# Copying and storing the last 128-token groups one at a time, on two DMA queues

## The chip, the cores and the metric

One core of one Trainium2 chip. The metric is the time of one execution in microseconds (us). Each run's time is about 1.8 us above the span that its trace shows, so the two are not mixed below: "time" is the metric, "span" is the trace. In the views PE is TensorE, PEld its weight loads, ACT ScalarE, DVE VectorE, POOL GpSimd and SP SyncE; a q behind a name (SPq, ACTq) is the sequencer of that engine, which issues DMAs and waits for semaphores.

## The reference, cut to what matters

```python
def _attn_ref(x):                      # x: 8 x 3008 x 256, f32
    X = np.fft.fft(np.fft.fft(x, axis=1), axis=2)
    return X.real
def _moe_ref(x, w_gate, w_val, w_out): # 24064 tokens, 256 -> 1536 -> 256
    gate = np.maximum(x @ w_gate, 0.0)
    val = x @ w_val
    return gate * val @ w_out
```

The kernel works in 24 blocks of tokens (8 batches, 3 blocks each). A block yields 512 tokens and, by the symmetry of the transform, 512 mirrored tokens. The output matmul handles them in groups of 128 tokens.

## The kernel before

The parts that matter. PSUM is the memory that TensorE writes its results to, in banks of 2 KB per partition. `pso` is a PSUM pool of two buffers; a tile `po` of 128 x 2 x 256 f32 (2 KB per partition, one bank) takes two groups, `s` even and `s` odd. `sg` is 0 for the plain half of a block and 1 for the mirrored one.

```python
pso = ctx.enter_context(tc.tile_pool(name="pso", bufs=2, space=PS))
...
def out_piece(t, half):
    b, blk, f = steps[t]
    for k in range(8 * f + 4 * half, 8 * f + 4 * half + 4):
        gi, ff = divmod(k, NF)                       # NF = 12 matmuls per group
        sg, s = divmod(gi, 4)
        g = 3 - s if sg else s
        if s == 0 and ff == 0:
            state["os"] = op.tile([128, 4, D], F32, tag="os", name="os")
        if s % 2 == 0 and ff == 0:
            state["po"] = pso.tile([128, 2, D], F32, tag="o", name="po")
        po, os_ = state["po"], state["os"]
        nc.tensor.matmul(po[:, s % 2, :], lhsT=..., rhs=wo[:, ff, :],
                         start=(ff == 0), stop=(ff == NF - 1))          # L539
        if s % 2 == 1 and ff == NF - 1:
            nc.scalar.copy(os_[:, s - 1:s + 1, :], po[:])               # L542
        if s == 3 and ff == NF - 1:
            store(b, blk, sg, os_)

def store(b, blk, sg, os_):                          # four stores, all on SyncE
    for u in range(4):
        ka = NKA * u + 4 * blk
        src = os_[32 * u:32 * u + 32].rearrange("p g d -> p (g d)")
        ...
        lo = 1 if ka + 3 == 47 else 0
        hi = 3 if ka == 0 else 4
        row = b * S + NA - ka - 3 + lo
        nc.sync.dma_start(out=view(out, row * D, [[NA * D, NB], [1, (hi - lo) * D]]),
                          in_=src[:, lo * D:hi * D])                    # L557
```

The framework that builds the program inserts the semaphores. It orders accesses of different engines to one PSUM tile, and the DMAs of SyncE and ScalarE take their completion semaphore in turn from one set of eight, whichever of the two queues they are on. A DMA is issued only when the DMA that had its semaphore before has landed.

## Time and profile before

| kernel before | |
|---|---|
| time, first 3 runs | 660.69 us median (660.03 to 661.86) |
| span of the profiled run | 660.6 us |
| TensorE busy | 637.0 us, 96% |
| after the last output matmul | 4.9 us |

First the head of the page: the busy time of each engine, and the first line of the chain that ended last.

```profile
span 660.6 us, 12759 instructions
...
PE 637.0 (96%) x4266; PEld 410.1 (62%) x4266; DVE 553.3 (84%) x871; ACT 426.7 (65%) x809; POOL 468.8 (71%) x630
...
PE 81%; POOL 11%; DVE 5%; issue 2%; ACT 1%; POOLq 0%; DVEq 0%
```

TensorE (PE) is the limit of the kernel: nearly always busy, and most of the chain. The change does not touch what it does in the body of the program. It acts at the end, so here is the timeline of the end. Columns: start, duration, engine, line and operation, output and input, count of merged instructions, and in brackets the idle time before the first of them with what ended it.

```profile
644.85 0.36 PE L521 MATMUL V<-pq,wm 128*128 128x480 bf16 x1
...
645.05 10.64 PE L539 MATMUL po<-wo,h 128*128 128x256 bf16 x96
...
653.16 0.58 ACT L542 COPY os<-po 128x512 f32<-128x512 f32 x1 [2.08 <-PE po L539]
655.73 0.58 ACT L542 COPY os<-po 128x512 f32<-128x512 f32 x1 [1.99 <-PE po L539]
656.34 1.72 SPq L557 DMA_DIRECT2D out_dram<-os  x4
```

All the work that remains after 645.05 us is 96 output matmuls, which run as one unbroken row to 655.7. A copy of 128x512 follows, then four stores that SyncE (SP) issues one after another. How their packets moved is in the windows of that stretch (window, its length, busy time of each engine, granted clock, share of the DMA engines, GB/s):

```profile
656.32:657.16 0.84, 0.00 (x0) 0.00 (x0) 0.00 (x0) 0.00 (x0) 0.00 (x0) 1.00 0.00 0
657.16:659.27 2.11, 0.00 (x0) 0.00 (x0) 0.00 (x0) 0.00 (x0) 0.00 (x0) 1.00 0.91 233
659.27:660.60 1.33, 0.00 (x0) 0.00 (x0) 0.00 (x0) 0.00 (x0) 0.00 (x0) 1.00 0.00 0
```

Last, the closing of the program: SyncE checks one semaphore after another, then drains, and all engines shake hands. The line of its drains:

```profile
L642 SPq DRAIN  x3: 7/7/7, 659.8 to 660.1; - x3
```

The first drain came at 659.8 and the end at 660.6; this last 0.84 us is the same in every trace below.

**A yardstick for what follows.** Runs of one kernel differ by 2 to 3 us (those of own_banks below by 4.9), which is more than this tail can yield. In the traces of kernels that differ only in the tail, the start of the last L521 matmul (the last line of work before the row of 96) lies anywhere from 642.9 to 645.8 us. So I read the *tail* of each trace: from the start of that matmul to the end of the span. Before it is 660.6 - 644.85 = 15.75 us.

### The profile page before, as it was taken

The numbers are of one execution on the slowest core, as the hardware profiler recorded it, in microseconds if no ns is written. First come the engines' busy times: TensorE is split into PE (matmuls) and PEld (weight loads), VectorE is DVE, ScalarE is ACT, GpSimd is POOL, SyncE is SP. The second block draws the span as 40 slices with busy tenths as digits, with TensorE's granted clock in tenths as the row PEclk, the third lists the DMA queues.
The fourth block names the chain that finished last, engine by engine and source line by source line (L and its number), as shares of the span: only waits on it lengthen the run. The fifth ranks groups of instructions, "written<-read, shape, count | busy, mean of one in ns | idle before, by whom it ended". The sixth has DMA issues, their size and how long they took to land.

```text
span 660.6 us, 12759 instructions
## 1 busy us (share of the span) xinstructions
PE 637.0 (96%) x4266; PEld 410.1 (62%) x4266; DVE 553.3 (84%) x871; ACT 426.7 (65%) x809; POOL 468.8 (71%) x630
## 2 busy tenths in 40 slices
PE   6789999999999999999999999999999999999997
PEld 3424666665666666666666666666656666666665
DVE  9857688888788887989888887988979898899991
ACT  5465676775667766676676766676666766666662
POOL 9639579959975599658995599756996355455451
PEclk9799999999999999999999999999999999999999
DMA  9792472393126721196114922177111241211113
GB/s 252 239 202 51 127 202 78 85 234 104 42 78 142 192 82 49 41 196 190 40 53 106 226 81 69 51 161 221 41 42 49 67 118 39 81 33 43 51 32 94
DMA packets 32294, 70.76 MB, mean 107 GB/s; under 512 B 4475, under 2 KB 21491, under 8 KB 30227
## 3 DMA queue, kind: packets, MB, share of 16 engines
q1 hardware_dynamic: 29892, 58.16, 32.3%
q0 software_dynamic: 2336, 11.80, 9.0%
q8 instruction: 33, 0.54, 0.3%
q14 instruction: 33, 0.26, 0.1%
HBM read 39.77 MB, written 30.96 MB: 107 GB/s over the span
## 4 chain that ended last, share of the span: by engine, by line
PE 81%; POOL 11%; DVE 5%; issue 2%; ACT 1%; POOLq 0%; DVEq 0%
PE po L539 33%; PE V L495 9%; PE V L493 8%; PE G L472 8%; PE G L471 8%; PE G L483 8%; POOL h L509 3%; POOL eo L102 3%; POOL xl L99 2%; PE V L521 2%; PE ps L162 2%; POOL eo L130 2%; DVE E L503 1%; PE psw L261 1%; PE ps L204 1%
## 5 line engine op out<-in xcount | busy, mean ns | idle before, releaser
L509 POOL TENSOR_TENSOR h<-gm,E 128x480 bf16<-128x480 f32 (+1 forms) x225 | 276.0, 1227 | 147.5 <-DVE E L517 128.2
L539 PE MATMUL po<-wo,h 128*128 128x256 bf16 x2304 | 333.5, 272 | 0.0
L539 PEld LDWEIGHTS <-h 128*128 128x128 bf16 x2304 | 222.7, 98 | 88.2 <-issue 3.9
L486 ACT ACTIVATE gm<-G 128x480 f32<-128x480 f32 (+1 forms) x288 | 167.3, 581 | 141.8 <-PE G L483 112.1
L497 DVE TENSOR_TENSOR h<-gs,V 128x512 bf16<-128x512 f32 x288 | 193.9, 686 | 32.6 <-PE V L495 22.0
L503 DVE SCALAR_TENSOR_TENSOR E<-nb,af,V 128x480 f32<-128x480 bf16 (+1 forms) x225 | 163.0, 724 | 16.4 <-PE V L493 10.5
L473 ACT ACTIVATE gs<-G 128x512 f32<-128x512 f32 x288 | 171.5, 595 | 0.8 <-PE G L472 0.8
L517 DVE SCALAR_TENSOR_TENSOR E<-E,V 128x480 f32<-128x480 f32 (+1 forms) x225 | 148.1, 658 | 0.0
L483 PE MATMUL G<-pq,wm 128*128 128x480 bf16 (+1 forms) x288 | 106.6, 370 | 7.8 <-ACT gs L473 7.7
L495 PE MATMUL V<-pq,ws 128*128 128x512 bf16 x288 | 109.0, 378 | 1.1 <-DVE E L503 0.5
L472 PE MATMUL G<-pq,ws 128*128 128x512 bf16 x288 | 109.1, 379 | 0.4 <-DVE pq L209 0.4
L471 PE MATMUL G<-pq,wc 128*128 128x512 bf16 x288 | 109.1, 379 | 0.0
L493 PE MATMUL V<-pq,wc 128*128 128x512 bf16 x288 | 109.1, 379 | 0.0
L542 ACT COPY os<-po 128x512 f32<-128x512 f32 x96 | 56.2, 586 | 58.4 <-PE po L539 58.4
L509 DVE TENSOR_TENSOR h<-gm,V 128x480 bf16<-128x480 f32 (+1 forms) x63 | 41.9, 665 | 39.3 <-ACT gm L486 33.8
L102 POOL TENSOR_TENSOR eo<-xl 94x381 bf16<-94x381 f32 x70 | 69.0, 992 | 0.4
L99 POOL TENSOR_TENSOR xl<-xl,xh 94x765 f32<-94x765 f32 x35 | 63.2, 1806 | 2.7
L495 PEld LDWEIGHTS <-ws 128*128 128x128 bf16 x288 | 28.1, 98 | 33.9
L472 PEld LDWEIGHTS <-ws 128*128 128x128 bf16 x288 | 28.1, 98 | 31.5 <-issue 0.2
L172 ACT CAST t<-ps 96x512 bf16<-96x512 f32 x63 | 36.9, 585 | 6.6 <-PE ps L160 5.4
L493 PEld LDWEIGHTS <-wc 128*128 128x128 bf16 x288 | 28.1, 98 | 14.8 <-issue 7.0
L471 PEld LDWEIGHTS <-wc 128*128 128x128 bf16 x288 | 28.1, 98 | 13.1 <-issue 9.7
(106 smaller groups left out, 346.0 us busy)
## 6 DMA issues: line engine op xcount, KB each, us to landing
out_dram<-os SPq DMA_DIRECT2D x176, 128.0 KB
xl<-in_x_dram SPq DMA_DIRECT2D x7, 1360.0 KB
Td<-t SPq DMA_DIRECT2D x7, 768.0 KB
t<-Td SPq DMA_DIRECT2D x7, 768.0 KB
nb<-Nd SPq DMA_DIRECT2D x24, 128.0 KB
xl<-in_x_dram SPq DMA_DIRECT2D x7, 238.0 KB
xl<-in_x_dram SPq DMA_DIRECT2D x4, 384.0 KB
xh<-in_x_dram SPq DMA_DIRECT2D x4, 384.0 KB
```

Of the source, the lines that this page charges most:

```text
L471: nc.tensor.matmul(e["G"][:], lhsT=wc[0][:, fs], rhs=pq[:, 0, :], start=True, stop=False)
L472: nc.tensor.matmul(e["G"][:], lhsT=ws[0][:, fs], rhs=pq[:, 1, :], start=False, stop=True)
L473: nc.scalar.activation(e["gs"][:], e["G"][:], ACTF.Relu)
L483: nc.tensor.matmul(e["G"][:, cols], lhsT=wm[0][:, f * 128:(f + 1) * 128], rhs=pqt[b, blk][:, 1, cols], start=False, stop=True, skip_group_ ...
L486: nc.scalar.activation(e["gm"][:, cols], e["G"][:, cols], ACTF.Relu)
L493: nc.tensor.matmul(e["V"][:], lhsT=wc[1][:, fs], rhs=pq[:, 0, :], start=True, stop=split(t))
L495: nc.tensor.matmul(e["V"][:], lhsT=ws[1][:, fs], rhs=pq[:, 1, :], start=False, stop=True, skip_group_check=split(t))
L497: nc.vector.tensor_tensor(e["h"][:, 0, :], e["gs"][:], e["V"][:], op=ALU.mult)
L503: nc.vector.scalar_tensor_tensor(e["E"][:, cols], nbt[b, blk][:, cols], af[:, f:f + 1], e["V"][:, cols], op0=ALU.mult, op1=ALU.add)
L509: eng.tensor_tensor(free(e["h"][:], 512 + cols.start + NB - 1, [NB, (cols.stop - cols.start) // NB], [-1, NB]), e["gm"][:, cols].rearrange ...
L517: nc.vector.scalar_tensor_tensor(e["E"][:, cols], e["E"][:, cols], 2.0, e["V"][:, cols], op0=ALU.mult, op1=ALU.subtract)
L539: nc.tensor.matmul(po[:, s % 2, :], lhsT=ht[t - f + ff]["h"][:, sg, g * 128:(g + 1) * 128], rhs=wo[:, ff, :], start=(ff == 0), stop=(ff == ...
```

## The change

Intent: shorten what follows the last matmul. The last 128 tokens need not wait to be copied and stored together with the 384 before them, and two engines can issue the stores faster than one.

```diff
-            if s % 2 == 1 and ff == NF - 1:
+            if ff < NF - 1:
+                continue
+            if t - f == len(steps) - NF and sg == 1:
+                nc.scalar.copy(os_[:, s:s + 1, :], po[:, s % 2:s % 2 + 1, :])
+                store_last(b, blk, os_, s)
+                continue
+            if s % 2 == 1:
                 nc.scalar.copy(os_[:, s - 1:s + 1, :], po[:])
-            if s == 3 and ff == NF - 1:
+            if s == 3:
                 store(b, blk, sg, os_)
+
+    def store_last(b, blk, os_, s):
+        for u in range(4):
+            ka = NKA * u + 4 * blk
+            if s == 0 and ka + 3 == 47:
+                continue
+            (nc.sync if u % 2 else nc.scalar).dma_start(
+                out=view(out, (b * S + NA - ka - 3 + s) * D, [[NA * D, NB], [1, D]]),
+                in_=os_[32 * u:32 * u + 32, s, :])
```

More of the change, by code (lines that the diff above doesn't have):

```diff
@@ L540, in out_piece @@
                              rhs=wo[:, ff, :], start=(ff == 0), stop=(ff == NF - 1))
-            if s % 2 == 1 and ff == NF - 1:
+            if ff < NF - 1:
[5 more added lines that the diff above has]
+            if s % 2 == 1:
                 nc.scalar.copy(os_[:, s - 1:s + 1, :], po[:])
-            if s == 3 and ff == NF - 1:
+            if s == 3:
                 store(b, blk, sg, os_)
+    def store_last(b, blk, os_, s):
[4 more added lines that the diff above has]
+            (nc.sync if u % 2 else nc.scalar).dma_start(
+                out=view(out, (b * S + NA - ka - 3 + s) * D, [[NA * D, NB], [1, D]]), in_=os_[32 * u:32 * u + 32, s, :])
     def store(b, blk, sg, os_):
```

## The prediction

> **What bounds the kernel now.** TensorE. The page has PE busy 96% of a 660.6 us span, and 81% of the chain that ended last is PE. In the windows from 560 to 640 us PE is always busy, at a granted clock of 1.00. The change leaves that alone. It acts only on the mirrored half of the last block, after about 650 us.
>
> **That tail before (timeline of the last 20 us).** 96 output matmuls run without a pause, one per 0.109 us (12 per group of 128 tokens, 1.31 us). The last ends at 655.71. One copy of 128x512 takes 0.585 (655.73 to 656.32). SyncE issues four stores of 128 KB in 1.72 us (656.34 to 658.06). Their packets run from 657.16 to about 659.2, the wait for the fourth ends at 659.64, the closing handshake at 660.6. So 4.9 us follow the last matmul: copy 0.6, stores 3.3, closing 1.0.
>
> **What the change does to it.**
> - *Shorter last copy.* 128x256 in place of 128x512. ACT's forms 128x480 and 128x512 differ by 27 ns for 32 columns (0.84 ns each), so I estimate 0.37 us: **-0.21**.
> - *Fewer issues behind it.* Two on each of two queues, not four on one. Starts on SyncE were 0.36 to 0.46 apart; the last issue now starts about 0.4 instead of 1.31 after the copy: **-0.9**.
> - *Less data behind it.* 128 KB, not 512; each store 32 KB. The fourth store took 2.0 us from issue to landing; the one-row store to Nd released its reader 1.1 us after its issue. I estimate 1.6: **-0.4**.
> - *New waits of TensorE.* Each pair of groups shares one PSUM tile of one bank. Until now the copy came after both. Now the copy of group 0 reads the bank before the matmuls of group 1 write its other half, likewise 2 and 3. The Trainium skill (PSUM — Partial Sum Buffer, "PSUM bank collisions raise a hardware error") says that two engines must be kept apart per bank and quadrant, not per address, so I expect the second group to wait for the copy. The trace before has no such wait on po. Cost: the last matmul starts at 655.42 and lands at 655.71 (0.18 more than its pitch), copy 0.37, release of PE about 0.05 (seen for gs): about 0.62 each, twice, both on the only chain: **+1.24**.
> - *More issues*, 15 stores of 1 KB rows instead of 4 of 4 KB: the first 11 hide behind later matmuls. A first use of ScalarE for stores has no trace here: **+0 to 0.3**.
>
> The skill (DMA: Bandwidth & Descriptors, "Issuing engines are not separate DMA queues") says that a second issuing engine saves only issue time, all I credit it with. -1.5 and +1.3 to +1.5 cancel: about -0.2 us. The whole tail after the last matmul is 0.7%, so 2% can't come from here.
>
> **Predicted: 660.5 us, 659.1 to 661.6 in 8 of 10. Faster by over 2%: 0.005; within 2%: 0.99; slower: 0.005.**
>
> **What would show it.** Two idle gaps of PE of about 0.6 us before an output matmul, released by the ACT copy; last matmul ending near 656.95; copies of about 0.37; last copy ending near 657.3; two issues per queue within 0.9 us of it; last landing about 2 us after the copy (3.3 before). Everything before about 648 us the same.
>
> **What would make it wrong.** No gap (halves not ordered): then about 659.2. ScalarE's issues slow, its queue's first use costly, or stores waiting for earlier ones' semaphores: up to 661.5. Runs differ by 1.8 us anyway.

## The result, and the profile after

| | before | after |
|---|---|---|
| time, median of 6 runs | 661.28 us (660.03 to 662.0) | 661.12 us (660.25 to 661.8) |
| ratio | | 0.9995, 95% interval 0.9979 to 1.0012 |
| tail in the trace | 15.75 us | 15.9 us |

A ratio is the mean time of one kernel's runs over the mean of the other's runs of the same rounds, so it is not quite the ratio of the medians.

No difference in time can be seen. The profiled run of the changed kernel has a span of 658.8 us, 1.8 us less than the one of before, but that is not the change: it had reached the last L521 matmul 1.98 us earlier. The head of its page:

```profile
span 658.8 us, 12777 instructions
...
PE 636.7 (97%) x4266; PEld 409.9 (62%) x4266; DVE 552.7 (84%) x871; ACT 426.7 (65%) x811; POOL 468.8 (71%) x630
...
PE 74%; POOL 11%; DVE 6%; DMA 4%; issue 3%; ACT 1%; SPq 0%; POOLq 0%; DVEq 0%; ACTq 0%
```

Busy times are those of before. The 4% of DMA in this chain come mostly from one load of x at 282 us, where the backward walk took another branch; the change is nowhere near it. The end is what differs:

```profile
642.87 0.36 PE L521 MATMUL V<-pq,wm 128*128 128x480 bf16 x1
...
643.08 6.71 PE L539 MATMUL po<-wo,h 128*128 128x256 bf16 x60
...
649.87 0.37 ACT L544 COPY os<-po 128x256 f32<-128x256 f32 x1 [0.77 <-PE po L539]
650.27 0.89 ACTq L558 DMA_DIRECT2D out_dram<-os  x2
650.29 2.78 PE L539 MATMUL po<-wo,h 128*128 128x256 bf16 x24 [0.50 <-ACT os L544]
...
652.32 3.97 SPq L558 DMA_DIRECT2D out_dram<-os  x7
653.11 0.37 ACT L544 COPY os<-po 128x256 f32<-128x256 f32 x1 [0.94 <-PE po L539]
...
653.53 1.47 PE L539 MATMUL po<-wo,h 128*128 128x256 bf16 x12 [0.46 <-ACT os L544]
...
655.04 0.37 ACT L544 COPY os<-po 128x256 f32<-128x256 f32 x1 [1.56 <-PE po L539]
655.44 0.87 ACTq L558 DMA_DIRECT2D out_dram<-os  x2
```

The row of 96 matmuls is broken twice: 60, then 24, then 12. Each break is ended by the copy of the first group of a pair (`<-ACT os L544`). The bracket says 0.50 and 0.46 because it counts from the modelled end of the matmul before; from start to start the breaks are 0.776 and 0.732, and the usual pitch is 0.109, so they cost 0.667 and 0.623, **1.29 us** together.

Two more lines. The waits of SyncE over the last 20 us (who waited for what: us in total, times, longest), and its drains:

```profile
SPq L558 <- DMA out_dram<-os: 2.6, 4, 1.4
```

```profile
L657 SPq DRAIN  x3: 7/7/7, 657.9 to 658.2; - x3
```

The first says that stores waited for *earlier stores to land*: they share the eight semaphores. Such waits were not there before, where the only waits of SyncE for a store were those of the closing. The second is the closing, to which I return.

So the sum of the tail, taken from the single records of both traces (us):

| piece | before | after | difference |
|---|---|---|---|
| L521 to end of last copy | 11.46 | 12.53 | +1.07 (waits of PE +1.29, shorter copy -0.21) |
| end of last copy to last landing | 3.32 | 2.08 | -1.24 |
| last landing to SyncE's first drain | 0.13 | 0.43 | +0.30 |
| drain to end | 0.84 | 0.84 | 0 |
| tail | 15.75 | 15.88 | +0.13 |

"Landing" is the moment at which SyncE's wait for that store's semaphore is released. (From the rounded lines shown above, the tail after is 658.8 - 642.87 = 15.93; the records give 15.88.) The +0.30 has a plain cause: at the end SyncE checks the eight semaphores in a fixed order at about 0.06 us each. Before, the store that landed last was last but one in that order; after, it was second, and six checks of long-finished stores followed it.

### The profile page after: what moved, and what is told of

Same layout as the page of the kernel before. It is cut to its first block, busy times and chain, and to the rows that moved or that the text cites. A ratio compares the mean times of both kernels' runs of the same rounds, so it can differ in the third digit from the quotient of the medians. Undisturbed runs are those within 1.5% of the kernel's fastest.

```text
span 658.8 us, 12777 instructions
## 1 busy us (share of the span) xinstructions
PE 636.7 (97%) x4266; PEld 409.9 (62%) x4266; DVE 552.7 (84%) x871; ACT 426.7 (65%) x811; POOL 468.8 (71%) x630
## 4 chain that ended last, share of the span: by engine, by line
PE 74%; POOL 11%; DVE 6%; DMA 4%; issue 3%; ACT 1%; SPq 0%; POOLq 0%; DVEq 0%; ACTq 0%
PE po L539 30%; PE V L495 8%; PE V L493 7%; PE G L472 7%; PE G L471 7%; PE G L483 7%; POOL h L509 4%; POOL eo L102 4%; DMA xh<-in_x_dram,ix 3%; POOL xl L99 3%; PE V L521 2%; PE ps L162 2%; DVE E L503 1%; DVE h L497 1%; PE psw L261 1%
```

## The experiments

The theory: the change does shorten what follows the last copy, and the copies that split a pair give it back, because both groups of a pair lie in one PSUM bank. (A bank of its own always means a tile of its own here, so no run separates the bank from the tile; "bank" below stands for both.) Rivals: the breaks cost nothing because the stores set the end; the stores gain nothing because their transfers are at a floor; the copies cost by their number and not by the bank. Except where a full timing is given, only tails are compared. The parts of all the tails stand together at the end of this section.

### copies_only: the cost alone

Against the changed kernel:

```diff
-                store_last(b, blk, os_, s)
+                if s == 3:
+                    store(b, blk, sg, os_)
```

> The cost side alone: the four single copies of the change, but the old four stores of 128 KB on SyncE after the last. The tail is read from the start of the last value matmul on wm (PE V, 15.75 us before the end in the kernel before, 15.93 in the changed one). Theory (a copy makes TensorE wait because both groups of a pair lie in one PSUM bank): two PE gaps of 0.62 to 0.67 us beyond the pitch, last copy 0.37, stores as before: tail 15.75 + 1.29 - 0.21 = 16.8. Rival (the gaps are swallowed, the end is set by the stores' own pace): tail 15.5 to 15.8.

Tail 16.83 us, as the theory had it. Both breaks are there, and the four stores behave as in the kernel before (last landing 3.33 us after the copy). Timeline:

```profile
652.15 2.78 PE L539 MATMUL po<-wo,h 128*128 128x256 bf16 x24 [0.51 <-ACT os L544]
...
655.39 1.47 PE L539 MATMUL po<-wo,h 128*128 128x256 bf16 x12 [0.46 <-ACT os L544]
...
656.90 0.37 ACT L544 COPY os<-po 128x256 f32<-128x256 f32 x1 [1.56 <-PE po L539]
657.29 1.71 SPq L573 DMA_DIRECT2D out_dram<-os  x4
```

The breaks lie on the only chain there is: they move the end by their full length, less 0.21 for the shorter copy.

### own_banks: the cost taken away

Against the changed kernel, a PSUM tile for each of the last four groups:

```diff
-            if s % 2 == 0 and ff == 0:
+            if ff == 0 and (s % 2 == 0 or (sg == 1 and t - f == len(steps) - NF)):
```

> The change, with a PSUM tile of its own for each of the last four groups. Bank theory: no PE wait for a copy, last matmul 1.29 us earlier than in the change relative to the anchor (10.8 instead of 12.1 us after it). If only the bank matters the tail is 15.93 - 1.29 = 14.6. Second theory, from the list of waits in the program: the 15 stores share 8 completion semaphores in turn over both queues, and with the groups 1.3 us apart the two last stores on SyncE have to wait for landings of stores that ScalarE issued 0.4 us or less earlier (the very last one for a store of its own group), so the last landing comes about 3.3 us after the last copy instead of 2.1 and the tail is 15.6 to 15.9, the gain lost again. Times: within 0.3% of before in either case.

Tail 15.62. Time 660.71 us median (660.14 to 665.05), before 661.33 on the same chip, ratio 0.9998 (0.9973 to 1.0023): no difference. The 96 matmuls are one row again, so the bank was the cause of the breaks, and the last copy ends 1.27 us earlier than in the changed kernel, measured from L521. But the last landing now comes 3.09 us after it instead of 2.08. The timeline, and the waits of SyncE:

```profile
643.47 10.64 PE L539 MATMUL po<-wo,h 128*128 128x256 bf16 x96
...
649.52 1.72 SPq L566 DMA_DIRECT2D out_dram<-os  x4
...
650.67 0.91 ACTq L558 DMA_DIRECT2D out_dram<-os  x2
...
653.27 3.18 SPq L558 DMA_DIRECT2D out_dram<-os  x7
654.16 0.37 ACT L544 COPY os<-po 128x256 f32<-128x256 f32 x1 [0.93 <-PE po L539]
```

```profile
SPq L558 <- DMA out_dram<-os: 2.1, 2, 2.0
```

This is the size that the second theory of the expectation gave. The list of waits in the built program for the last two stores on SyncE is (output of the program listing, not of the profile; the number after DMAHW names one of the eight semaphores):

```
297 L558 DMACopy out_0_dram<-os_8984 32x256 [waits DMAHW0_49,Activation_49]
298 L558 DMACopy out_0_dram<-os_8984 32x256 [waits DMAHW1_49]
```

DMAHW1 had been given to the first store of the same group, which ScalarE issued at 0.03 us after the copy. SyncE was released from this wait at 1.60 us after the copy, when that store had landed, and only then issued the very last store. But the expectation had named only such waits at the end, and this one cost at most 0.2 us: the issue before it had ended at 1.41. The long wait, 2.0 us, came earlier. SyncE's first small store (of the first group) had the semaphore of a store of the same group that ScalarE had issued, the second of the two at 650.67, and could be issued, at 653.27, only when that one had landed. From then on SyncE issued its seven stores 0.42 to 0.57 us apart, so that those of the last group stood at the end of a full queue.

So most of the gain of 1.29 us was lost again: 1.01 us of later landing, through waits for shared semaphores and the queue that the first of them backed up. No run removes the early wait alone.

### own_banks_3_1: fewer stores, so fewer waits for semaphores

As own_banks, with the first three groups stored together after group 2 (four stores of 3 KB rows), the last one alone:

```diff
                 nc.scalar.copy(os_[:, s:s + 1, :], po[:, s % 2:s % 2 + 1, :])
-                store_last(b, blk, os_, s)
+                if s >= 2:
+                    store_last(b, blk, os_, 0 if s == 2 else 3, s + 1)
```

(`store_last` here takes a range of groups, as in pair_copies below.)

> As own_banks, but the first three groups are stored together (four stores of 3 KB rows after group 2), the last group alone: 8 stores instead of 15, so no store of the last group waits long for an earlier one (at most about 0.2 us for one). Both theories of own_banks together: no PE wait, last landing about 2.1 to 2.3 us after the last copy, tail 14.6 to 15.0, 0.7 to 1.1 us less than before (0.1 to 0.17% of the time, so perhaps not clear of noise). If semaphores don't matter it equals own_banks.

Tail 15.00, at the edge of what was expected. Last landing 2.54 us after the copy: one store on SyncE still waited 0.7 us for an earlier one, more than the 0.2 that I had worked out. Time 661.64 us median (660.95 to 662.4), ratio 0.9999 (0.9983 to 1.0015): timing does not resolve it.

### pair_copies: the benefit alone

Against the changed kernel:

```diff
-                nc.scalar.copy(os_[:, s:s + 1, :], po[:, s % 2:s % 2 + 1, :])
-                store_last(b, blk, os_, s)
+                if s % 2 == 1:
+                    nc.scalar.copy(os_[:, s - 1:s + 1, :], po[:])
+                    store_last(b, blk, os_, s - 1, s + 1)
...
-    def store_last(b, blk, os_, s):
+    def store_last(b, blk, os_, s0, s1):
...
-            if s == 0 and ka + 3 == 47:
-                continue
+            lo = s0 + 1 if s0 == 0 and ka + 3 == 47 else s0
             (nc.sync if u % 2 else nc.scalar).dma_start(
-                out=view(out, (b * S + NA - ka - 3 + s) * D, [[NA * D, NB], [1, D]]), in_=os_[32 * u:32 * u + 32, s, :])
+                out=view(out, (b * S + NA - ka - 3 + lo) * D, [[NA * D, NB], [1, (s1 - lo) * D]]),
+                in_=os_[32 * u:32 * u + 32, lo:s1, :].rearrange("p g d -> p (g d)"))
```

> The benefit side without the split of the copies: one copy of 128x512 per pair as before, four stores of 2 KB rows per pair, alternating between the two queues. No PE wait (matmuls as before). Last landing about 2.2 to 2.5 us after the copy instead of 3.3, closing up to 0.3 longer: tail 14.7 to 15.1. Rival (the queue and the size gain nothing because the transfers are at their floor): tail 15.6 to 15.8.

The end in the timeline:

```profile
655.58 0.59 ACT L545 COPY os<-po 128x512 f32<-128x512 f32 x1 [1.99 <-PE po L539]
656.19 0.85 ACTq L558 DMA_DIRECT2D out_dram<-os  x2
```

Tail 14.85: without a single copy more than before, the two queues and half the bytes bring the last landing to 2.18 us after the copy. The rival that says the stores are at a floor is out. Time 660.72 us median (659.41 to 661.73), ratio 0.9984 (0.9967 to 1.0001), not clear of 1.

### queues_only and one_queue: which half of the benefit?

The prediction had credited -0.9 us to fewer issues per queue and -0.4 to fewer bytes, as two terms that add. These two runs do one part each. queues_only, against the kernel before (stores of 128 KB, two queues):

```diff
-            nc.sync.dma_start(out=view(out, row * D, [[NA * D, NB], [1, (hi - lo) * D]]),
+            q = nc.scalar if (b == B - 1 and blk == NBLK - 1 and u % 2 == 0) else nc.sync
+            q.dma_start(out=view(out, row * D, [[NA * D, NB], [1, (hi - lo) * D]]),
```

> The kernel before with one thing of the change: the last four stores (128 KB each) alternate between ScalarE and SyncE. If the issue time is what counts, as the prediction had it (-0.9), last landing about 2.4 us after the copy, tail 14.9 (plus up to 0.3 of closing). If the bytes count (512 KB moved in 2.0 us at a nearly full DMA share in the kernel before), landing 3.0 to 3.2 after the copy, tail 15.4 to 15.7.

Tail 15.96, *longer* than before by 0.2 and outside what either theory expected, though on the side of the bytes. Timeline, and the windows after the copy (which ended at 657.29):

```profile
657.31 0.78 SPq L558 DMA_DIRECT2D out_dram<-os  x2
657.31 0.85 ACTq L558 DMA_DIRECT2D out_dram<-os  x2
```

```profile
657.29:658.13 0.84, 0.00 (x0) 0.00 (x0) 0.00 (x0) 0.00 (x0) 0.00 (x0) 1.00 0.07 15
658.13:660.25 2.12, 0.00 (x0) 0.00 (x0) 0.00 (x0) 0.00 (x0) 0.00 (x0) 1.00 0.89 226
```

The issues are over in 0.85 us instead of 1.72, and the packets still run from 0.84 to 2.95 us after the copy, as they did from one queue (0.84 to 2.96). 480 KB took the DMA engines 2.1 us at 89 to 91% busy either way. Issue time was not what this tail waited for. Why the last wait was released at 3.47 instead of 3.32 to 3.38 is not settled.

one_queue, against the changed kernel (stores of 32 KB, SyncE alone):

```diff
-            (nc.sync if u % 2 else nc.scalar).dma_start(
+            nc.sync.dma_start(
```

> The change with all 15 stores on SyncE. The last of the four issues starts 1.1 to 1.2 us after the last copy instead of 0.46, each still lands 1.6 after its issue: last landing 2.7 to 2.8 us after the copy, PE gaps unchanged (1.29), tail 16.4 to 16.7. If the second queue is worth nothing: tail 15.9.

Tail 17.40, last landing 3.59 us after the copy. I had expected 16.4 to 16.7 and had counted only the issues of the last group. The timeline shows what I missed:

```profile
650.44 1.72 SPq L566 DMA_DIRECT2D out_dram<-os  x4
...
652.25 6.89 SPq L558 DMA_DIRECT2D out_dram<-os  x15
```

15 stores at 0.46 us each take 6.89 us. SyncE issues almost without a pause from 650.44 to 659.14, and is still busy with stores of the third group when the last copy ends at 656.73. So here the stores of 32 KB were limited by issue, and those of 128 KB by bytes.

The four combinations, by the last landing after the last copy (us):

| | one queue | two queues |
|---|---|---|
| large stores (before's) | 3.32 | 3.47 |
| small stores (the change's) | 3.59 | 2.08 |

Neither part gains anything alone. Only both together gain 1.24. Each number is of one trace, and the small stores are also more stores (15 for 4).

### shared_everywhere and own_everywhere: the cost magnified

To lift the PE waits out of the noise and out of the drained end of the program, both kernels copy one group at a time in *all* blocks, with before's stores. The first against the kernel before; the second against the first:

```diff
-            if s % 2 == 1 and ff == NF - 1:
-                nc.scalar.copy(os_[:, s - 1:s + 1, :], po[:])
+            if ff == NF - 1:
+                nc.scalar.copy(os_[:, s:s + 1, :], po[:, s % 2:s % 2 + 1, :])
```

```diff
-            if s % 2 == 0 and ff == 0:
+            if ff == 0:
```

> The cost magnified: every pair of groups in every block is copied one group at a time out of its shared PSUM bank (192 copies of 128x256 for 96 of 128x512), stores as before. Bank theory: at each of 96 places the second group waits for the copy, 0.62 us less what other matmuls stand between (0.2 in most steps), plus what the copy waits for ScalarE: 0.3 to 0.8 us each, 30 to 80 us in all (690 to 740 us). Rival (the wait is a feature of the drained end of the program, where nothing else runs; in the stream it hides): within 1% of before.

> As shared_everywhere, but each group has a PSUM tile of its own (two buffers in turn). Same number and size of copies, 15 us more of ScalarE in all, so if the copies themselves cost, this is as slow as shared_everywhere; if it is the shared bank, within 1% of before (660 to 667 us).

shared_everywhere: 695.51 us median (694.91 to 696.27), before 661.78 on the same chip, ratio 1.0508 (1.0486 to 1.0530). own_everywhere: 660.07 us (657.82 to 661.24), ratio 0.9973 (0.9942 to 1.0005). Head of TensorE's list of waits, first with shared banks, then with own ones:

```profile
PE po L539 <- ACT os L542: 29.8, 95, 0.5
```

```profile
PE G L483 <- ACT gs L473: 7.3, 8, 1.1
```

With shared banks TensorE waits 95 times for a copy. With own banks that wait is gone from the list; what leads it then was there before (7.7 us in the kernel before). The number and the size of the copies are the same in both, so it is the shared bank (or tile) that costs, 34 us over 96 places, 0.35 us each on average; in mid-stream some of each wait hides behind other work.

### own_2_2, own_all_2_2, own_everywhere_2, before_again

own_2_2 is pair_copies with own banks and single copies; own_all_2_2 does the same in all blocks:

```diff
-            if s % 2 == 0 and ff == 0:
+            if ff == 0 and (s % 2 == 0 or (sg == 1 and t - f == len(steps) - NF)):   # own_2_2
+            if ff == 0:                                                              # own_all_2_2
...
-                if s % 2 == 1:
-                    nc.scalar.copy(os_[:, s - 1:s + 1, :], po[:])
+                nc.scalar.copy(os_[:, s:s + 1, :], po[:, s % 2:s % 2 + 1, :])
+                if s % 2:
                     store_last(b, blk, os_, s - 1, s + 1)
...
-            if s % 2 == 1:                                                           # own_all_2_2
-                nc.scalar.copy(os_[:, s - 1:s + 1, :], po[:])
+            nc.scalar.copy(os_[:, s:s + 1, :], po[:, s % 2:s % 2 + 1, :])
```

own_everywhere_2 and before_again are own_everywhere and the kernel before once more.

> Looking for a version that beats both: single copies out of own PSUM tiles (no PE wait, last copy 0.37 us), stores per pair of groups as in pair_copies (2 KB rows, alternating queues). In its list of waits no store of the last pair waits for one of the last pair or of the two groups just before, so the last landing should be as in pair_copies, 2.2 us after the last copy. Tail 14.85 - 0.21 = 14.6 to 14.7, the shortest so far; 1.1 us less than before, 0.17% of the time, which timing may not resolve.

> own_2_2 with single copies out of own PSUM tiles in all blocks (own_everywhere, which was 0.27% faster than before in 3 rounds, 95% interval -0.58 to +0.05%). Tail 14.6 to 14.7. If the 0.27% was real and not only its 0.2 us of tail, the ratio to before is about 0.996; if it was noise, about 0.998.

> own_everywhere once more, with more rounds and on the same chip as the others of this call: tail 15.55 again (last copy 0.21 shorter, all else as before). Ratio to before 0.9997 if only the tail counts, about 0.997 if the body gained.

> The kernel before against itself, as a gauge of noise: ratio 1.000 with an interval of about 0.2% on each side; tail 15.75 within 0.1 us. If its tail moves by more than 0.1, the comparisons of tails are less sure than they look.

| against before (661.76 us median of 11 runs) | time, median | ratio, 95% interval | tail |
|---|---|---|---|
| before_again | 661.50 us (660.86 to 663.14) | 1.0003 (0.9989 to 1.0017) | 15.80 |
| own_2_2 | 660.73 us (659.61 to 661.93) | 0.9991 (0.9978 to 1.0004) | 14.62 |
| own_everywhere_2 | 659.55 us (658.93 to 661.76) | 0.9975 (0.9960 to 0.9990) | 15.59 |
| own_all_2_2 | 658.79 us (657.37 to 659.95) | 0.9950 (0.9938 to 0.9963) | 14.63 |

The end of own_2_2:

```profile
652.78 0.37 ACT L544 COPY os<-po 128x256 f32<-128x256 f32 x1 [0.94 <-PE po L539]
654.09 0.37 ACT L544 COPY os<-po 128x256 f32<-128x256 f32 x1 [0.94 <-PE po L539]
654.50 0.85 ACTq L558 DMA_DIRECT2D out_dram<-os  x2
```

The copies follow at the pace of the matmuls (1.31 us), and the issues at once. Tail 14.62, 1.13 less than before, as expected; by itself that is 0.17% and timing alone does not separate it from nothing. own_all_2_2 is faster than before clear of noise, by 0.5%, and is the version to keep. Of its 0.5%, 0.17% is the tail. The rest agrees with own_everywhere, which was 0.25 to 0.27% faster in both calls with only 0.2 us of tail (clear of noise in the second call alone). Where in the body that comes from I have not settled: between the 61st gate matmul and the last, the two traces of own_everywhere show 474.0 and 474.3 us and own_all_2_2 475.0, but the two traces of the kernel before show 477.3 and 475.7 and differ among themselves by as much.

All tails (us; the four pieces add up to the tail):

| kernel | L521 to end of last copy | to last landing | to first drain | to end | tail |
|---|---|---|---|---|---|
| before | 11.46 | 3.32 | 0.13 | 0.84 | 15.75 |
| after | 12.53 | 2.08 | 0.43 | 0.84 | 15.88 |
| copies_only | 12.54 | 3.33 | 0.13 | 0.84 | 16.83 |
| own_banks | 11.26 | 3.09 | 0.43 | 0.84 | 15.62 |
| own_banks_3_1 | 11.25 | 2.54 | 0.37 | 0.84 | 15.00 |
| pair_copies | 11.47 | 2.18 | 0.37 | 0.84 | 14.85 |
| queues_only | 11.47 | 3.47 | 0.19 | 0.84 | 15.96 |
| one_queue | 12.54 | 3.59 | 0.43 | 0.84 | 17.40 |
| own_2_2 | 11.25 | 2.17 | 0.37 | 0.84 | 14.62 |

Last digits can be off by 0.01 through rounding.

## Why the prediction was right or wrong

The predicted time (660.5 us, range 659.1 to 661.6; "within 2%" at 0.99) held: 661.12 us, with no difference from before that timing can see. A time in this range is no test of the mechanism: own_banks (660.71) and pair_copies (660.72), which each lack a part of it, lie in it too, and so does the kernel before (661.28). The tails are the test. There the mechanism held, term by term, with three faults.

- **TensorE bounds the kernel and the tail is too small for 2%: right.** After the last matmul 4.9 us remained of 660.6, and no version of the tail moved the end by more than 1.7 us.
- **New waits of TensorE, +1.24: right.** Two breaks, 0.667 and 0.623 us, 1.29 together. own_banks removed them by a bank of its own for each group and nothing else, and shared_everywhere against own_everywhere shows the same cause with 34 us at stake. This rested on the Trainium skill (PSUM — Partial Sum Buffer, "PSUM bank collisions raise a hardware error"), whose rule is to guard PSUM "by bank × quadrant (by bank is the simple version), not by address". The traces agree that the program was ordered this way: disjoint halves of one bank, and a wait at both places (95 waits at 96 places in shared_everywhere). Whether the program orders by bank or by tile no run shows. No run here let two engines collide, so that an error would be raised is not shown.
- **Shorter last copy, -0.21: right.** 0.585 to 0.372 us.
- **Stores behind the copy, -0.9 for issues and -0.4 for bytes: right for the path of the last store, wrong as two separate gains.** Measured -1.24 against -1.3. On the path of the store that lands last both terms can be read: its issue starts 0.46 instead of 1.31 us after the copy (-0.85), and it lands 1.62 instead of 2.01 us after that (-0.39). But neither is to be had without the other. Two queues alone gained nothing (3.47 us against 3.32), small stores alone gained nothing (3.59), both together gained 1.24. The step that failed is "the last issue now starts about 0.4 instead of 1.31 after the copy: -0.9" as a gain in its own right: in the kernel before, the packets of 480 KB kept the DMA engines 91% busy for 2.1 us, and an earlier issue only put stores in line behind them. The Trainium skill (DMA: Bandwidth & Descriptors, "Issuing engines are not separate DMA queues") says that DMAs of all issuing engines run on the same 16 DMA engines and that a second issuing engine saves only issue time; for the large stores the runs agree, and there the issue time saved was worth nothing. I also wrote 128 KB for each of the four; the fourth is 96.
- **A term that was missing, +0.30.** Nothing in the prediction stood for SyncE's final checks, one semaphore after another at 0.06 us. It is most of why the tail grew by 0.13 us where the prediction had it shrink by 0.2.
- **"No gap: then about 659.2": wrong.** That is, without the breaks it foresaw about 1.5 us of gain. own_banks has no gap and a tail only 0.13 us shorter than before. The prediction named "stores waiting for earlier ones' semaphores" only as a thing that might add time; in own_banks it is the next limit behind the PE waits: 1.01 us of later landing, together with the queue that these waits back up.
- **Cost of ScalarE's first stores, 0 to 0.3: none seen.** ScalarE's issues took 0.39 and 0.44 us behind the last copy, SyncE's 0.31 and 0.41.

So the large change in the order of the end moved the time little for this reason: 1.45 us of gain (copy and stores) were paid with 1.29 us of new waits of TensorE and 0.30 us of a longer closing.

## What to carry to other kernels

Before splitting a PSUM evacuation into smaller pieces, look at which bank the next piece is being written to: a piece per bank cost nothing here, two pieces in one bank cost a full copy with its latencies, 0.62 to 0.67 us at each pair at the end (5% of the time when done throughout). A second DMA queue helped here for stores of 32 KB, which one queue could not issue fast enough (15 in 6.89 us), and did nothing for stores of 128 KB, which already kept the DMA engines busy. When many small stores share a few completion semaphores, count how many are in flight: a store can end up waiting for one of its own group to land.

## What the Trainium skill lacked or had wrong

- DMA: Bandwidth & Descriptors, "Issuing engines are not separate DMA queues": it says that the sequencer time saved by a second issuing engine "is usually small relative to the DMA itself". For stores of 32 KB it was not small: an issue took 0.31 to 0.44 us, where the last store landed 1.6 us after its issue began; 15 issues on SyncE alone took 6.89 us, and the second queue brought the last landing from 3.59 to 2.08 us after the last copy. For stores of 128 KB it was so (3.32 and 3.47 us).
- DMA: Bandwidth & Descriptors, "Why a DMA increments its semaphore by 16 and not by 1": it asks for one semaphore per in-flight slot, and does not say what a small set of them costs in waiting. Here eight served both queues in turn, and SyncE waited up to 2.0 us in own_banks for an earlier store to land before it could issue.
- PSUM — Partial Sum Buffer, "PSUM bank collisions raise a hardware error": it gives the rule but no price. Here one ordered copy of 128x256 between two groups of matmuls in one bank cost TensorE 0.62 to 0.67 us when nothing else was there to run, and 0.35 us on average in mid-stream.
- No page has the price of the semaphore checks with which this program closes: 0.06 us for each semaphore that SyncE checks, in a fixed order (0.13 to 0.43 us from the last landing to the first drain, by the place of that store in the order), and then 0.84 us in all traces.
